# Odd rows of keys and queries copied inside SBUF, the first batch's value rows sent in two chunks, the first tokens by batch, a scaling moved to ScalarE, and a new order

## The chip, the cores and the metric

One core of a Trainium2 chip runs the kernel. The metric is the device time of one execution in microseconds (us); the time before is the median of three runs. The profile shows one further execution. Engines are named as the profile names them: PE (TensorE matmul), PEld (its weight load), DVE (VectorE), ACT (ScalarE), POOL (GpSimd) and SP (SyncE, which here issues every DMA).

## The reference

A gated linear recurrence with a complex decay, for 4 batches, 8 heads, 768 tokens and a head width of 48, followed by a two-layer network over the 3072 tokens:

```python
mag = np.sqrt(a_re * a_re + a_im * a_im)
scale = np.minimum(mag, 0.999) / (mag + 1e-06)
a_re_n, a_im_n = (a_re * scale, a_im * scale)
for t in range(S):
    ar, ai = (a_re_n[:, :, t, :, None], a_im_n[:, :, t, :, None])
    new_re = ar * S_re - ai * S_im
    new_im = ar * S_im + ai * S_re
    kv = np.einsum('bhd,bhe->bhde', k[:, :, t], v[:, :, t])
    S_re, S_im = (new_re + kv, new_im)
    y[:, :, t] = np.einsum('bhd,bhde->bhe', q[:, :, t], S_re)
# x = y as (4 * 768, 8 * 48)
h = x @ w_in                                     # 384 -> 2048
g = np.maximum(h, 0.0) + alpha * np.minimum(h, 0.0)
out = g @ w_out                                  # 2048 -> 384
```

## The kernel before

The recurrence is cut into 24 units of 128 tokens (4 batches of 6 chunks). The work is written as 15 + 24 generator tasks, each of which issues one instruction, or a small group, per step; a string of letters, `ORDER`, says which task takes the next step. So the order of every engine's queue, SP's included, is written out by hand in that string, and each engine runs its queue strictly in that order.

- A to I, `gates(g, b, c0, c1)`: from a_re and a_im the magnitude and phase of the decay for 128 tokens (g = 0), 256 tokens (g = 1) or 384 tokens (g = 2 to 8, 1152 elements in each of 128 partitions). It begins with L280, a scaling on DVE, and L282 to L286 on ACT; it goes on with products on DVE (L288 to L294), running sums (L307), more on both engines, and sends the phases to DRAM (L333, tensor phs) and, after L357 and the products of L367, the decays (L370, tensor decs).
- J, `loads`: for each unit the tile KQ. Its 96 partitions hold each of the 48 dimensions twice, in an even and in an odd row, so q and k are loaded twice from DRAM, with a step of two partitions: L508 (q) and L510 (k), 192 KB each, four loads a unit. Then PP from phs (L516) and T from decs, one load for the even rows and one for the odd (L523). KQ has three buffers, T two, PP one.
- K, `half_rows`: DRAM to DRAM copies of v with the rows apart that three of the levels need (tensor vsc, L489), six of 288 KB for each batch, each for all six chunks. L, `loads_v`: the tiles V (L532 to L537) and VL (L556 from v, L560 from vsc).
- M, `pieces`: the first token's keys of all batches (`start`, L405, single elements), alpha (L408), which DVE turns into al_1 at L410, and the weights as they come, in 16 pieces. N and O, `weights`: the pieces are 64-bit numbers that ACT (L444 to L448) and DVE (L452, L454) make into 32-bit ones.
- P to m, `unit(u)`: on DVE the rotation by the phases (L588, L590), then per level the decays (L646; the first of the six reads T and the rotated tile WQ, the others read T), on ACT copies of operands (L669, L685), on PE the small products (L605), masked on DVE (L629) or ACT (L619); then the state (L717 to L740; the first state of a batch at L654 reads `start`), and y on PE (L755, L769), which ACT copies out at L777. Units 0 and 1 go straight on to the network's tile xT (L786, L791); the others go through DRAM (L800, tensor ysc, and L817).
- n, `loads_x`; o, `all_mlp`: the network, 12 blocks of 256 tokens. Blocks 0 and 1 run plainly (L837 into L844 on ACT, L846 on DVE, L887); block 0 starts on unit 0's tokens alone. From block 2 on: L859 into L868 and L872 on ACT and L874 on DVE, then the seven products of a Strassen-like scheme (L977), whose weight combinations DVE makes at L943 and L952.

Of the kernel before, what the change touches and what calls it, by code (L numbers as in the profile page):

```python
# [27 lines left out]


ORDER = (  # L30
    "AAAAAMBMJMMBABABAAAAAAAAAAAAAJMBAAABBBMJJBAABAAKAAMAAAAAAAAAAAAABBBBNBBOBBBBBOBBONOJLOPBPPJLPJLLBBBL"
    "BNBPBBBBNBBBOBBBBPOPPPPJOPOPPPPBNNJLLJCCJJMBMKCPPNPCOCPQCKCNPJNNNPNPCQJLCPNPPPPPPPPPPPCQCCCCCNCPCQKL"
    "LKKMQQQPQLLLLOLJJJJJMCCNCCOOQQOCNNNQPPPPPPPPPQQQPCQCCLMQOQRPLLLLJoQooJMCLLLLCLCCCNRCoQooQoNRCCCCQoOQ"
    "QQQQooCooCQooNoDQRROoRCORRQQOQQDLLLRRLNLQDMJoCJOJQCCNRDNJQRRQQQOROOoQQQNOLLLOJLRRRDDDLoLooooooooQRRD"
    "QQooRRRRRRDNQooooRooRLJoLJooLRRDoNooooLoLRDRMRSRooDDSoooooooooooDoSDooooRLLRoLDSDRROSSSOoooooooLoOOS"
    "RRJSSOJJMRNoooooNooRJMSJLSSDoSNoooRooooSSSooooRooooOSDLLLLLMRSLRSSoDooooSSSSOSSoSoooOTOoooSSDOTooooo"
    "oooSSNSSDLNNNNNNNLooNNooSSMOLLLLLLJJOJJSoSSSJJoooSSSSSTLLJLnoooooooDLLTDJDOKTToTOooooooTTTLLODoooooT"
    "ooLDTTToLToDoDDDooooooooJJJJJooToTTTooDoUTTDUoLooTLoDLDDooUETTTLLLTToTooooJoTToTDTDDDTUEUUUUUUDDETTT"
    "ToooooUooEooTTTTTTETTUUooooULUVUUoLoooooooooUUoooUVUEUVLJJUJEVoJLooooooooUVUJUVUEooooLLLJLKJLKLVVVoV"
    "oUooVEooooooVooUooEUUUVVELUKLLVEVEoULUooooUUooEKKKKKUUWooVVVULUUULLoLLoooLVoVVEVJEoooJoLEVVVVoVVLLVE"  # L40
    "LooonLLLLoooEoVoLoVVWVEooJooooEJJJJVWKVEVVVWWWWEoWEWWWoVooVoVVVVVVoWLLWWWWELoWooooooooJooooooooLJLLL"
    "WWWWoEWLELJLoEooEWLLLWWooWWWoLLoooEXJEXXWoWoooWooXWWJXWWEWWXooooooooooooXXEXJJooXooWooWFFEEEEEEEEXoo"
    "ooooWooooooWWooWWXWXXXoooooooXLLooooooooLooooXJFoJXXLXXXXXXooYYYooooooXXXLooooooXoXooXYoYYYoonYKLLLL"
    "LLLLLLoYJYXXJXXoooooooYooooooooooooooooYFJYXXYoooXFJJKFFoooXooKXooXLLoYYYLoFXXXLXLLooooooFoFLFLoKYYY"
    "YYYYYLLLLLLJZoooooZooooooooJooYoYYFoLooYoooFYoYYoFFYFFFFFFFZYooooooooooYJoooYYoFYoFFYZFoJJJooJYooFYY"
    "YYYoZZZLLoooLooZJoooZZFJaZooooooooooLLZZZaFFFFooonoZZaZFFFaGooLLooooooooooooooooooooooooZZaZZZZZaFaZ"
    "ZaoooLooGJLLLLLoooooLLZZoJoooooZaZoooZJoZFGZaZooaoGJFGGFFFJFooooooooooooooZoZGZGoZoooZGGooooKooZooZZ"
    "ZLZZoooooooooooabaaGLLbaobLoGoooaLoooooaLLLLooooooLoooGaGaaoaaaaaGoooooooooooaaKoJJJobbooJLLaaLaoooo"
    "obGabbaaaaooLoobGbJbGGJbaoooJoaoaoobaaaaacoobbbbbooGbooooLcoooooooooobbbbbbbGooobJJbooLLLLLooncLLLLb"
    "boLooooooboooooobbGLLbbLGcooooGoooKocLJcJJJJGGGGGccbGbcbbcooooooooooGooooooooooooocGobooooboooobcccb"  # L50
    "bcdbbboooooooooooooooooocLLoooooccccooooooJLGooococccoJJLLLLHLLcccJcLLLLLLoooocooccddGdGdcHdcccccHGG"
    "GGodHoodoooooooooGGJoooHddoodoooooooooooocococoJcccccLdoJLJJJJJodddddooHHHoooooooooooooooodddddddddo"
    "ooeooeHoooeodHodooooooooLooooooodooooLJddddddeeedeendooLLoHHHLLLLLLLLHHHHLeeoooooooooooooooooooooood"
    "ooooedHededeedddJLLLdooooooooooooooooooooLeeeeHeooeooeeLLeHLLooooooooofeeeeoooeooLHJeeofeeHeooLLLLLe"
    "HoJHHLoooooJJJJJooHoHHeeHHoooeoffooooefeffHeeeeefffooofoooooooooJooLooooHffLooffffooooJoooooooooogoH"
    "oofffooffnHJooJHgHgfffLfooooooffIHJooooooLLLLLooooooooooHofgfoooooLLLLHLLHLHHfffgJgffffgggoooooooooo"
    "ooooJfooooooooofoooIgogfooooooIofgfgfffgooooooohgIggoooooooooIoooogIgoooogggIgIggJgooghgJooooLoooohh"
    "ooooohoooooggLLLLLLLLooggghhhhhooLJooIohooohLLLJLhggIooogoIgooJJJghhggggghonihIIooJJoooIooooooooohho"
    "ooooIoLLKLLooooooooooihhhJoJhhhhhIoIooIooIooohIohooooooooooLooooohhJiLhoooooooooLooooooooooooooiLLLL"
    "LLLLooohhihiIiiioJJhiiohhhohohooohiihLLLLLLihhiiiooooLooooooiiihihiiLLLLiiioooooooooooooiijooooiioIo"  # L60
    "ooooioooJoLLLLJooiiiiiIIiooooJjiIIIJJIIIIIooooooojoojoooooooJooooioooooJoiooojojjjIiiIIIoijiioooInjo"
    "ooooIoooooooooLjIIIkooooooooooLLLLLJLLLLojjjjjoooooJooooojoooooooLjjjoooooooooooooJoojjjjjjjkooooojo"
    "jjoooooooooJLoooookooojjjkkkjkjkLLjkjkLooooojoooJkjojJkkjjjLLjjJLLLLJkJLLkkoooooooooookkkkkkoookkooo"
    "okkoooookLLLLLLkooooookkoLookoolkkklollooooJokooJoooooookkJJJllkolllllookoooooooooooooookllkokkkklll"
    "LlooooooooooollllllLlloooooooolommonlJJlmoooooooooLLLLLooooooooooooooooooLLLLLLLloooooollllLlmoloooo"
    "oooooooooollmommlooolmmooolmmmmmlloommmoooooooooooooLLLLoooolmmmmoooloLLLLLLoommmmlooomomLLmoooooLLo"
    "ooooooooooooommooomommooooommoooooomomoomommmmmnoooooooooooooooooooooooooooooooooooooooooooooooooooo"
    "oooooooooooooooooooooooooooooooooooooooooooooooooooooooooooooooooooooooooooooooooooooooooooooooooooo"
    "oooooooooooooooooooooooooooooooooooooooooooooooooooooooooooooooooooooooooooooooooooooooooooooo")
# [28 lines left out]
def kernel(  # L98
# [145 lines left out]
    def gates(g, b, c0, c1):  # L244
# [35 lines left out]
        nc.vector.tensor_scalar(out=d, in0=x, scalar1=1.5, scalar2=TINY, op0=ALU.mult, op1=ALU.add)  # L280
# [119 lines left out]

    def pieces():

        t = yield DMA(8)
        with nc.allow_non_contiguous_dma(reason="one token"):
            nc.sync.dma_start(start[0:D2:2], kv_in[:, :, :, 0].rearrange("b d h -> d b h"))  # L405
        done["start", 0] = t
        t = yield DMA(8)
        nc.sync.dma_start(al_1, alpha)  # L408
# [68 lines left out]
    def half_rows():  # L477

        one = NCH * D2
        for b in range(B):  # L480
# [12 lines left out]
    loaded = {}

    def loads():
        for u in range(NU):
# [4 lines left out]
            n = min(P, S - 1 - c * P)
            if n < P:
                nc.gpsimd.memset(KQ[:, 1, :, n:P], 0.0)
            for i in range(2):
# [5 lines left out]
                nc.sync.dma_start(KQ[rows, 1, :, 0:n], kv_in[b, :, :, c * P + 1:c * P + 1 + n])  # L510
# [650 lines left out]
```

## Time and profile before

| what | value |
|---|---|
| time before, median of 3 runs | 763.77 us (761.33 to 764.42) |
| time of the profiled execution | 760.66 us |
| its span, first to last instruction | 758.6 us |
| PE busy | 682.7 us (90% of the span) |
| DVE busy | 605.5 us (80%) |
| ACT busy | 491.5 us (65%) |
| DMA packets | 175548, 129.82 MB, mean 171 GB/s |

The span is what the profile shows; 2.1 us of the profiled execution's time lie around it. A busy PE is not a PE at its peak: its matmuls are pipelined. The views used are the page, the table of busy times by stretch of the span, the waits (who waited for whom), the groups of instructions by line and shape, and the timeline of one engine.

### The profile page before, as it was taken

The page shows a single profiled execution, that of the slowest core. Times are in us where ns is not written, and L with a number is a line of the kernel's source. Part 1 is how long each engine was busy: PE and PEld are TensorE (multiplying, and loading weights), DVE is VectorE, ACT ScalarE, POOL GpSimd, SP SyncE. Part 2 cuts the span into 40 slices and gives each one's busy share as a digit, 9 for nine tenths or more (in the row PEclk, how much of TensorE's full clock was granted, in tenths as well). Part 3 has the DMA queues.
Part 4 walks back from the last instruction along what each step waited for, and adds up shares of the span by engine and source line. Part 5 has one row for each costly group of instructions (what it writes and reads, how often), then busy time and mean ns, then how long its engine had stood idle before and what let it go on. Part 6 is the DMA issues. An engine that isn't in the chain of part 4 may idle for free.

```text
span 758.6 us, 26858 instructions
## 1 busy us (share of the span) xinstructions
PE 682.7 (90%) x11752; PEld 581.3 (77%) x11752; DVE 605.5 (80%) x798; ACT 491.5 (65%) x887; POOL 13.0 (2%) x51
## 2 busy tenths in 40 slices
PE   0026789999999999999999999999999999999998
PEld 0015577776767888888888888988888988888987
DVE  6899999998999799998887997888876866742323
ACT  7979988965767678766856668565766455353330
POOL 5000000000000000000000000000000000000000
PEclk9998699999999999999999999999999999999999
DMA  9898999898678768667586648754744645211000
GB/s 243 252 318 242 283 242 224 217 267 232 189 187 232 219 158 179 206 187 160 140 207 203 172 91 217 218 127 118 191 122 141 190 113 143 74 45 52 1 22 21
DMA packets 175548, 129.82 MB, mean 171 GB/s; under 512 B 66184, under 2 KB 166792, under 8 KB 174984
## 3 DMA queue, kind: packets, MB, share of 16 engines
q1 hardware_dynamic: 175432, 128.12, 63.3%
q8 instruction: 92, 1.51, 0.8%
q14 instruction: 24, 0.20, 0.1%
HBM read 100.13 MB, written 35.02 MB: 178 GB/s over the span
## 4 chain that ended last, share of the span: by engine, by line
PE 70%; DVE 12%; DMA 7%; ACT 4%; SPq 4%; issue 3%; POOL 0%; DVEq 0%; ACTq 0%; POOLq 0%
PE ps_h L859 27%; PE ps_o L977 24%; PE ps_y L769 5%; PE ps_lv L605 5%; DVE KQ L646 3%; PE ps_y L755 2%; PE ps_kv L729 2%; DMA V<-in_v_dram 2%; SPq L556 2%; PE ps_kt L717 1%; DMA T<-decs 1%; DMA decs<-room 1%; PE ps_h L837 1%; PE ps_h L977 1%; DMA shared<-in_w_out_dram 1%
## 5 line engine op out<-in xcount | busy, mean ns | idle before, releaser
L859 PE MATMUL ps_h<-xT,w_in_sb 128*128 128x256 f32 x960 | 232.3, 385 | 0.0
L859 PEld LDWEIGHTS ps_h<-xT,w_in_sb 128*128 128x128 f32 x960 | 175.1, 190 | 21.9
L646 DVE TENSOR_TENSOR KQ<-KQ,T 96x1024 f32<-96x1024 f32 x120 | 145.9, 1216 | 31.9 <-PE ps_lv L605 25.4
L977 PE MATMUL ps_o<-w_out_sb,shared 128*128 128x192 f32 x624 | 113.1, 331 | 0.4 <-ACT top L993 0.4
L868 ACT ACTIVATE shared<-ps_h 128x512 f32<-128x512 f32 x80 | 47.8, 598 | 98.5 <-PE ps_h L859 98.2
L874 DVE TENSOR_TENSOR shared<-shared,ps_h 128x512 f32<-128x512 f32 x80 | 54.5, 682 | 68.6 <-ACT shared L872 68.6
L977 PEld LDWEIGHTS ps_o<-w_out_sb,shared 128*128 128x128 f32 x624 | 101.8, 190 | 3.4 <-ACT top L993 0.7
L977 PE MATMUL ps_o<-shared 128*128 128x192 f32 x448 | 84.0, 333 | 0.0
L872 ACT ACTIVATE shared<-shared,al 128x256 f32<-128x256 f32 x160 | 73.7, 502 | 2.4
L977 PEld LDWEIGHTS ps_o<-shared 128*128 128x128 f32 x448 | 72.8, 190 | 3.1 <-DVE top L1004 0.2
L605 PE MATMUL ps_lv<-WQ 96*32 96x32 f32 x2304 | 34.7, 202 | 38.6 <-DVE WQ L588 29.9
L605 PEld LDWEIGHTS ps_lv<-WQ 96*32 96x32 f32 x2304 | 26.3, 115 | 52.9 <-DVE WQ L588 29.9
L669 ACT COPY WQ<-KQ 96x1024 f32<-96x1024 f32 x48 | 49.8, 1039 | 26.2 <-DVE KQ L646 25.9
L769 PEld LDWEIGHTS ps_y<-A,VL 64*48 64x48 f32 x2304 | 39.9, 122 | 21.1 <-issue 17.6
L887 PE MATMUL ps_o<-w_out_sb,shared 128*128 128x384 f32 x128 | 52.5, 513 | 1.4 <-DVE shared L846 1.4
L769 PE MATMUL ps_y<-A,VL 64*48 64x64 f32 x2304 | 52.1, 225 | 1.7 <-DMA VL<-vsc 1.7
L837 PE MATMUL ps_h<-xT,w_in_sb 128*128 128x256 f32 (+1 forms) x240 | 52.3, 350 | 0.8 <-ACT xT L791 0.8
L837 PEld LDWEIGHTS ps_h<-xT,w_in_sb 128*128 128x128 f32 x240 | 41.1, 197 | 13.0 <-ACT xT L791 1.1
L685 ACT COPY W<-KQ 96x512 f32<-96x512 f32 x48 | 30.7, 640 | 26.4 <-DVE KQ L646 24.9
L619 ACT ACTIVATE A<-ps_lv,columns 128x64 f32<-128x64 f32 x144 | 36.8, 335 | 14.9 <-PE ps_lv L605 14.8
L777 ACT COPY T<-ps_y 48x512 f32<-48x512 f32 x48 | 27.8, 579 | 22.4 <-PE ps_y L769 21.7
L605 PE MATMUL ps_lv<-KQ,W 96*32 96x32 f32 x1536 | 24.3, 204 | 17.5 <-ACT W L685 17.5
(111 smaller groups left out, 962.7 us busy)
## 6 DMA issues: line engine op xcount, KB each, us to landing
T<-decs SPq DMA_DIRECT2D x48, 384.0 KB, 4.7
PP<-phs SPq DMA_DIRECT2D x24, 387.0 KB, 5.4
KQ<-in_q_dram SPq DMA_DIRECT2D x48, 192.0 KB, 5.6
phs<-room SPq DMA_DIRECT2D x14, 577.5 KB, 4.6
decs<-room SPq DMA_DIRECT2D x7, 1152.0 KB, 6.0
KQ<-in_k_dram SPq DMA_DIRECT2D x40, 192.0 KB, 4.8
vsc<-in_v_dram SPq DMA_DIRECT2D x24, 288.0 KB, 7.1
VL<-vsc SPq DMA_DIRECT2D x48, 144.0 KB, 3.9
```

The lines of the kernel that those rows point to most:

```text
L605: nc.tensor.matmul(t[64 * i + j:64 * i + j + HC // 2, p], lhsT=keys(n, g), rhs=queries(n, g), start=True, stop=True)
L619: nc.scalar.activation(a[:, :, cols], t[:, :, at:at + name], AF.Copy, scale=s)
L646: nc.vector.tensor_tensor(out=x, in0=x if x0 is None else x0, in1=m, op=ALU.mult)
L669: nc.scalar.copy(z.rearrange("p i n t -> p i (n t)").rearrange("p i (m h) -> p m i h", h=h), bass.AP(tensor=KQ.tensor, offset=KQ.offset + ...
L769: nc.tensor.matmul(o, lhsT=Vp[h][64 * i:64 * i + 64, s, e_ * D:(e_ + 1) * D], rhs=a, start=False, stop=(s == 1 and h == LEVELS[-1]))
L837: nc.tensor.matmul(p, lhsT=w_in_sb[:, f // 2, kk, f % 2 * P:(f % 2 + 1) * P], rhs=x_of[m][:, kk, c * P:(c + n) * P], start=(kk == 0), stop ...
L859: nc.tensor.matmul(p[:, i], lhsT=w_in_sb[:, f // 2, kk, i * P:(i + 1) * P], rhs=x_of[m][:, kk], start=(kk == 0), stop=(kk == NK - 1))
L868: nc.scalar.activation(gt, p, AF.Relu, scale=-1.0)
L872: nc.scalar.activation(some_, some_, AF.Copy, scale=al_1[:, f + i:f + i + 1])
L874: nc.vector.tensor_tensor(out=gt, in0=gt, in1=p, op=ALU.add)
L887: nc.tensor.matmul(sums[0], lhsT=gt, rhs=w_out_sb[:, f], start=(f == start), stop=(f == stop))
L977: nc.tensor.matmul(z, lhsT=a[:, i], rhs=w[:, i], start=i == 0, stop=i == F2 - 1)
```

## The change

Five edits:

- `loads`: for every unit but the first, only the even rows of KQ are loaded from DRAM (q and k, 192 KB each); when both have landed, one DMA of 384 KB copies the even rows to the odd rows inside SBUF.
- `half_rows`: for the first batch the copies are made for chunks 0 and 1 first and for chunks 2 to 5 later, twelve DMAs in place of six; units 0 and 1 then wait for the first six alone.
- `pieces`: the first token's keys are loaded for batch 0 alone at the start and for batches 1 to 3 after the second pair of weight pieces.
- `gates`: the scaling that opens a gate group is made on ACT, with the same result, for the seven groups g = 2 to 8.
- `ORDER` is another string, with 3878 letters in place of 3894.

```diff
-        t = yield DVE(N // 2, tx)
-        nc.vector.tensor_scalar(out=d, in0=x, scalar1=1.5, scalar2=TINY, op0=ALU.mult, op1=ALU.add)
+        if g < 2:
+            t = yield DVE(N // 2, tx)
+            nc.vector.tensor_scalar(out=d, in0=x, scalar1=1.5, scalar2=TINY, op0=ALU.mult, op1=ALU.add)
+        else:
+            t = yield ACT(N, tx)
+            nc.scalar.activation(d, x, AF.Identity, scale=1.5, bias=bias_tiny)
...
-        t = yield DMA(8)
-        with nc.allow_non_contiguous_dma(reason="one token"):
-            nc.sync.dma_start(start[0:D2:2], kv_in[:, :, :, 0].rearrange("b d h -> d b h"))
-        done["start", 0] = t
+        def first_tokens(b0, b1):
+            t = yield DMA(8)
+            with nc.allow_non_contiguous_dma(reason="one token"):
+                nc.sync.dma_start(start[0:D2:2, b0:b1], kv_in[b0:b1, :, :, 0].rearrange("b d h -> d b h"))
+            return t
+
+        done["start", 0] = yield from first_tokens(0, 1)
...
+            if f == 1:
+                t = yield from first_tokens(1, B)
+                for b in range(1, B):
+                    done["start", b] = t
...
-            for i, h in enumerate(SPREAD):
-                for s in range(HP // 2):
-                    rows = v[b, 2 * s]
-                    src = bass.AP(tensor=rows.tensor, offset=rows.offset + one, ap=[[2 * h * one, P // h], [1, h * one]])
-                    end = yield DMA(150)
-                    nc.sync.dma_start(vsc[s, i].rearrange("n (m h) c e -> (n m) (h c e)", h=h), src)
-            for c in range(NCH):
-                done["halves", b * NCH + c] = end
+            for c0, c1 in ((0, MC), (MC, NCH)) if b == 0 else ((0, NCH),):
+                for i, h in enumerate(SPREAD):
+                    for s in range(HP // 2):
+                        rows = v[b, 2 * s]
+                        src = bass.AP(tensor=rows.tensor, offset=rows.offset + one + c0 * D2,
+                                      ap=[[2 * h * one, P // h], [one, h], [1, (c1 - c0) * D2]])
+                        end = yield DMA(150)
+                        nc.sync.dma_start(vsc[s, i].rearrange("n (m h) c e -> (n m) h c e", h=h)[:, :, c0:c1].rearrange(
+                            "m h c e -> m h (c e)"), src)
+                for c in range(c0, c1):
+                    done["halves", b * NCH + c] = end
...
-            yield DMA(196, takes=(R["KQ"],))
+            tq = yield DMA(196, takes=(R["KQ"],))
...
-            for i in range(2):
+            for i in range(2 if u == 0 else 1):
...
                 nc.sync.dma_start(KQ[rows, 1, :, 0:n], kv_in[b, :, :, c * P + 1:c * P + 1 + n])
+            if u > 0:
+                t = yield DMA(393, tq, t)
+                nc.sync.dma_start(KQ[1:D2:2], KQ[0:D2:2])
...
-            k_ = yield DVE(H * D, k_, ("start", 0))
+            k_ = yield DVE(H * D, k_, ("start", b))
```

Counted in the two programs, SP issues 678 DMAs in place of 694 (KQ: 50 loads and 23 copies in place of 96 loads; vsc 30 in place of 24; `start` 2 in place of 1), DVE 791 instructions in place of 798 and ACT 894 in place of 887. PE issues the same matmuls in another order, which changes from one kind of matmul (a unit's small products, transposes, states, y, and the network's) to another 414 times in place of 425. Relative to the other queues' order, the first copy of y (L777) has on ACT one each of L444, L446, L448 and L685 less ahead of it, and one scaling more. On DVE, the first L874 has the same instructions ahead of it as before, less three L280.

More of the change, by code (lines that the diff above doesn't have):

```diff
@@ L36 @@
[L36 to L45, printed above, removed]
@@ L66 @@
[L66 to L67 removed]
+    "AAAAABMMAMBKMMBBAAAAAAAAABNMJJKAAAAAAAAJKJBBBAAAAAAAABMBAAAAALLAAAAAAJBBBBBBOBBBBBOBONOOBBPPKPPJJMBB"
+    "BBLLLLBBCNNNBPMBLBBBBPPPPPJLJNNBNPOOBNPNBCBBBPCJOPPPPPLOPOCCCNKPPPPPPPPPPPCCCLPPPPCJCCMNCJJKQPQCPQCC"
+    "COQCQQQJMLCPQCLLLLJNQCOOMKQKCCNNOPPPPPPJPPPJLQQCCPQQQKMLLLJJLCCCLCCONQQRRooooCooQQQNCooQoCooooNNRNLC"
@@ new lines @@
+    "CCLoQQQQQQQOORooooQooQoRRRMOJLRoQRQOLJDLLRLLLOQMNNNoooooooooRKoDDDoCCCJJQNNCRoQDDQQQQRQQRQRRDoRLoooD"
+    "QoooOoOOQoOOoQoRRooooLCRRRRLLLLLooRRooooLMoJoRRRSSooooRRooRRDNooJoRDDooooooooNNRSNNoDooRLoKLKLMLSORR"
+    "SooSOoSoooDLLLJJSSSMDooooooooNSRoooRSSNNNMRRoRJJRoRRooLLLLLDSSSoOLONSoOOooooooJSSJSoooooTSSLLSSSOLLL"
+    "LSSSSSoOLLLODToJoJSoDNNSOooTSTDNNDDSooooooooSDTTTTMSSSSSSSSSNSoLooTTOoooOooLDnOOOTooooooooooTTTLJDJT"
+    "JDDDLLLLLLTDJooooooooTDUDDLDLJJLLoooUooDoooTTTToTDooDDoooooooTTToTToDUDooTToToTTTTUUUUTTTDLLoooooUTo"
@@ new lines @@
+    "UUDDEJJooUToooTUDUTTTUooooUUUKDVLLLTTVEEELoooooooooEEoLUUUUUUUUooooLLLVoUUEEEooUoJVoooUUooooUoJUUEEo"
+    "ooooooooVEEEEEVEULLLLLLUVoVVoUUKKoKEJJVKKKUoJVVEoUUULooooooUUVVVVoooooVVVooLJLLooooooooVJJLLLLLLLVLL"
+    "LLVnooVVVVVVVVVooooJJoEWWoVVWEJVVVWWWWWWVVVooJoVVoVWEWWWVVVVVLLLoWoWEEWJJJJWoLLLLooooooooooooooooooo"
+    "oEWWWXXXELEEEEoWWLJLooooWWWWEoWWoooooooooooWooLooWLLLWWXoLXooXooooWWWEEEEEEoooEooooooXoXKJEFWWoooEoo"
+    "oooWoWoXooXXoWoWEWWWWXXXXYXoXooooooooooooooooooXLnJJXLLXXXooooLLXoooooYYoXXXXXoooooooKXoLLLLLFLLLXLL"
@@ new lines @@
+    "YooFoXXXXXJYYXXJKooYYFoYFoYoooooooooooooooFKFFXoJXoXXooJooXXFYLFXXooooooLooooYYJJYZYFYYooooooooooooo"
+    "FooooooooYJYYYFYYYYooYoZYFYoZooooooYooooooLLLKYLYYZoYYZLLLLLFFLLZFFZJZZFYFFFYFZYLLJJooooooooooooYoYo"
+    "YYYYYYFLLLLJLJooooooooFLLLnLFZFLooooooFFFZZZZaZZoooooooooooooooooaFLLoFZZZoooLooooooFFooZooooooZZZZZ"
+    "ZZoFoaFFooooooooGLLoZGJooJKZZZFZZFFoaaaaaZoZZKKooFooooooGoGGGaooZooooooaZoooooooooKaGoooooooJoZJaaFZ"
+    "ZKGaZZaaaobooooooooooooooooaaaoaaoGoGoZLGoLLLLaaaaobbooooooaooJJoooooooooaGLLabbooaLLLLLLbababaaaoob"
@@ new lines @@
+    "bbbGGobGoGooLooaoGooaoabbaGaaJJJJaaJooLbboGoooobnLbLLLooooooooooooobbbooobbGLJooobbbbbbocoGocbbLLLLL"
+    "LLLLGooooooooooGoooooobbbcbGJJGGGGbcoooooooooooJJGGooooooobGbcccoccGobcocooooooooooooGobcbcbbboLcccb"
+    "bcodHoooooooooooooooooocccdoccccooocoGGcoooHooooHJJGcoooGLLcooocHocooGdcccddLKdddcoHccJcddooHoooLoJo"
+    "LLLLLLJGoooooLLLLooGGooHHHHoooooooooooodcooHcoocdddcHHHdcccddcJoHooooooJLoLJoooooooooddLLodHHddddooo"
+    "JooHHeHHooLednLLLLedddoooLLLLoooooooooooooodooodLoLoodddeddHeeddeooHHHooooeHHoeeHooooooooooooooooooo"
@@ new lines @@
+    "odHJJooododHeeedeLeoooooooddddoooLJooooooLoooeeeeJJeeeoooHoooLLoHoooooofffoeeeoeeooeoeeLLLLLLLLLLooo"
+    "ofoooooooefJeeeJJeHHeeooooooooooooooooIefffeoofooooooooooooeffffIJfHHHeeeeeJfffoooooJooHnooooooooooo"
+    "oofffgofgIfoooofHffooofffoooLLgoHooooHoooJfoofLoLLLLIgIoooooooooLLLLoLLLLfffffggggffIooooJHooooooooo"
+    "JJoooooIgggfIoooooooooooooooooofgfgfffghhgoghgoooooooooffooooLLLooooLoggghIIggoJooooooooooooooooLLgJ"
+    "ggggJoooLLLgogIgooLLgghhhhLLLJgggJhJhhhIIIooooooooooooIoohgooIIghghgIhhIoggggoJJoJoooohooooonoIiiJLh"
@@ new lines @@
+    "LLooooooooooooooooooooIoooIiLLLLLLLLLLoooooiLooooooooohhhhhhhhiiiihooooooooooooooJhoooooohhioooooohh"
+    "LhhIihIIIIooohoooooIihhooooohIIiIhihohiiiihhohhLLoLoooooLiLiiiioooLoooooLooiiJJLoIooIIIIoiiioLLJJJoL"
+    "LLLoooooIIoooooooooooLIIoooooJjjoooooooooooooJooooiioojojiiiiojjiijiioooooIjoiooijoojoijjjjiiiiijjjn"
+    "LkoooooooooooooooLoLLLojjojjjjjjJLjLLLLLoLLLoooooojJjoJJooooooooooooooojjooooooooooooooooooooookokko"
+    "oooooooooojjjkkLjkjjjkkooJoooookkojojoojkkkJjjjjjkkkoooooooooolkkkkkkooookkoooLooLLoLLLLLLkkkooooooo"
```

31 lines of the change are left out of this document (5 added, 26 removed).

## The prediction

> **What bounds the kernel now.** I read the profile's page first, for the shape of the run, and then cut the span into the stretches that the page's digits suggest.
>
> ```profile
> span 758.6 us, 26858 instructions
> ...
> PE   0026789999999999999999999999999999999998
> ...
> DVE  6899999998999799998887997888876866742323
> ```
>
> Each digit is the busy share of 19 us. PE has next to nothing to do in the first 38 us and is full from about the seventh slice; DVE is full from the second slice to about the twelfth. The busy times by stretch (columns: length, then busy us and instructions of PE, its loads, DVE, ACT, POOL, then granted clock, DMA share, GB/s) put numbers on it:
>
> ```profile
> 0.00:76.00 76.00, 17.85 (x532) 15.19 (x532) 64.91 (x101) 65.56 (x91) 11.15 (x35) 0.96 0.91 263
> 76.00:100.00 24.00, 18.42 (x449) 14.59 (x449) 23.79 (x36) 23.67 (x37) 0.00 (x0) 0.76 0.97 291
> 100.00:260.00 160.00, 151.88 (x2822) 115.80 (x2823) 147.34 (x193) 115.42 (x220) 0.79 (x5) 1.00 0.86 225
> 260.00:700.00 440.00, 439.80 (x7649) 384.49 (x7648) 350.60 (x441) 274.48 (x518) 1.09 (x11) 1.00 0.58 150
> 700.00:759.00 59.00, 54.74 (x303) 51.25 (x301) 18.84 (x30) 12.38 (x25) 0.00 (x0) 1.00 0.04 14
> ```
>
> From 260 us on PE is busy 494.5 of 499 us, and the change takes no matmul away. So nothing that happens there to DVE, ACT or the DMAs can pay, except by harm; the end moves by as much as PE's full stretch moves to the left. PE stands idle 58.2 us before 76 us, 5.6 us from there to 100 us and 8.1 us from there to 260 us. In the same stretches DVE is busy 64.9 of 76, 23.8 of 24 and 147.3 of 160 us: the head is DVE's, with ACT as full beside it from 76 to 100 us. The hand-over lies where the network's later blocks begin, at the first L874 on DVE:
>
> ```profile
> 227.29 0.67 DVE L874 TENSOR_TENSOR shared<-shared,ps_h 128x512 f32<-128x512 f32 x1
> ```
>
> I therefore ask of each edit how much earlier it lets DVE reach this instruction, and whether it makes DVE wait on the way.
>
> **The scaling on ACT.** Its rows, with those of the ACT work that I need next (columns: count, busy us, mean ns, idle before):
>
> ```profile
> L280 DVE TENSOR_SCALAR room<-room 128x1152 f32<-128x1152 f32 x4 | 3.0, 748 | 0.0
> L319 ACT ACTIVATE room<-room,columns 128x1152 f32<-128x1152 f32 x3 | 3.8, 1256 | 0.0
> L444 ACT ACTIVATE top<-shared 128x768 f32<-128x768 f32 x16 | 14.4, 906 | 0.6 <-DVE w_in_sb L454 0.6
> L446 ACT ACTIVATE w_in_sb<-shared,columns 128x768 f32<-128x768 uint32 x8 | 7.9, 992 | 0.0
> L448 ACT ACTIVATE w_in_sb<-shared 128x768 f16<-128x768 f32 x8 | 8.5, 1068 | 0.1
> L685 ACT COPY W<-KQ 96x512 f32<-96x512 f32 x18 | 11.5, 641 | 12.2 <-DVE KQ L646 10.8 <-DVE room L367 1.3
> ```
>
> The instructions that stand on DVE ahead of the first L874 are the same in both orders but for three L280: 3 × 0.748 = 2.2 us off the engine that sets the head. ACT takes them as L319's kind, Identity with a bias: 3 × 1.256 = 3.8 us more. From 100 to 260 us ACT has 44.6 us free, so two of the three are covered; the one that falls in the full stretch up to 100 us costs between 0 and 1.3 us, and I take 0, since the order also takes ACT work out of that place. Without that cover the 2.2 us would shrink to about 0.9.
>
> **The order.** The first copy of y on ACT opens the network's work:
>
> ```profile
> 71.20 1.17 ACT L777 COPY T<-ps_y 48x512 f32<-48x512 f32 x2
> 76.25 0.79 PE L837 MATMUL ps_h<-xT,w_in_sb 128*128 128x128 f32 x2 [0.84 <-ACT xT L791]
> ```
>
> ACT's queue ahead of it loses one each of L444, L446, L448 and L685 and gains a scaling: 0.906 + 0.992 + 1.068 + 0.641 − 1.256 = 2.4 us. On DVE, the eighth L846 has one each of L292, L294, L588, L646, L737 and L740 less ahead of it, besides two scalings, so PE gets more of block 0's features before 100 us. But those six are only put behind, and the first L874 has them ahead of it again. What the order can win there is DVE's waiting, not its work. Between 0 and 2.4 us; I take 1.0 us, nearer the low end, since DVE has only 0.2 us of idle from 76 to 100 us.
>
> **The first tokens.** The start of SP's queue, and what waits for it:
>
> ```profile
> 1.83 0.73 SPq L405 DMA_DIRECT2D start<-in_k_dram  x1
> 2.60 1.16 SPq L272 DMA_DIRECT2D room<-in_a_re_dram  x1
> 3.81 0.48 SPq L408 DMA_DIRECT2D al<-in_alpha_dram  x1
> ```
>
> ```profile
> 4.99 0.52 ACT L286 ACTIVATE room<-room 128x384 f32<-128x384 f32 x1
> 7.10 0.17 DVE L410 TENSOR_SCALAR al<-al 128x16 f32<-128x16 f32 x1 [2.63 <-DMA al<-in_alpha_dram]
> ```
>
> L288, the first gate group's next step, was ready at 4.99 + 0.52 = 5.5 us but stands on DVE behind L410, which waits for alpha. With `start` for one batch issued behind a_re, alpha's turn on SP comes at about 1.83 + 0.48 + 0.73 = 3.0 us in place of 3.81: 0.8 us, and everything in the head follows from this group. The bounds are 0 (the second a_re then ends the wait) and 7.1 − 5.5 = 1.6 us; I take 0.8. The other batches' keys, and v in chunks, are wanted later or no sooner than before: the last of the six vsc DMAs that units 0 and 1 need stands at the same place of SP's queue as all six did, before unit 0's VL. I cost them at nothing; the cover is that place, and if it were gone PE's y would wait for one more DMA to land, up to the 7.4 us of the longest such landing quoted below.
>
> **The copy inside SBUF.** No such DMA is in this trace. T's load from the profile's page (issues, KB each, median us from issue to landing), and the landing times of all of KQ's loads:
>
> ```profile
> T<-decs SPq DMA_DIRECT2D x48, 384.0 KB, 4.7
> ```
>
> ```profile
> DMA to landing us min/median/max: 3.4/5.2/7.4
> ```
>
> ```profile
> 64.34 0.62 SPq L510 DMA_DIRECT2D KQ<-in_k_dram  x1
> 77.45 1.21 DVE L588 TENSOR_TENSOR WQ<-KQ,PP 96x1024 f32<-96x1024 f32 x1
> ```
>
> By its size the copy is nearest to T's load, 4.7 us; the bounds are KQ's own shortest and longest, 3.4 and 7.4 us. Unit 2 shows the cover: k issued at 64.34, landed 5.2 us later, copy issued in 0.62 us and landed 4.7 us after that is 74.9 us, 2.6 us ahead of L588; with 7.4 us it is 77.6 us, just late. So nothing is lost on DVE while k stands where it stood, and I take 0. If the cover is gone, L588 waits, and all of DVE's queue with it. SP issues two loads less and one copy more a unit, 0.62 us each; a gain from that is excluded in the full stretch by PE's 439.8 of 440 us. The Trainium skill's page "DMA: Bandwidth & Descriptors" (Anatomy of one DMA) fits 2.0 us plus bytes over 436 GB/s; for 384 KB that would be an estimate of 2.9 us, and the copy would land at 73.1 us, which leaves the sum as it is. No run shown here has this copy.
>
> **The sum.** 2.2 + 0.8 + 1.0 = 4.0 us earlier, from 760.66 us of the profiled execution (span 758.6) to 756.7. The median of the runs is 763.77, 3.1 us above that execution, and my forecast stands on the median: 759.8 us. With all terms at their ends it is from 757.6 (2.2 + 1.6 + 2.4) to 762.9 (0.9 alone). About 0.5%, 3.8 us, is what a measurement of this kernel can tell from no change, so the forecast itself lies at that edge.
>
> **Rivals.** First, slower: SP stops at each copy until q and k have landed, and what stands behind comes late.
>
> ```profile
> SPq L800 <- ACT T L777: 91.7, 33, 9.2
> ...
> SPq L523 <- DMA decs<-room: 8.7, 3, 6.6
> SPq L523 <- DMA ysc<-T: 8.0, 8, 2.9
> ...
> DVE KQ L646 <- DMA T<-decs: 6.0, 6, 2.2
> ```
>
> In 15 of the 23 units at most three issues stand between the load of k and the copy, so SP stops there for about 5.2 − 2 × 0.62 = 4.0 us. In 12 units the first load of T stands at most eight issues behind the copy. T comes just in time already: SP holds it for its buffer, and DVE has waited for it six times. If each of these 12 units lost 1 us of PE, the time would be 759.8 + 12 = 772 us. It decides where SP's stop runs past the moment at which T's buffer comes free. Against it: SP stands 91.7 us at L800 anyway, so the queue as a whole is not short of time. The Trainium skill's page "DMA: Bandwidth & Descriptors" (Rules for kernel authors) demands exactly this wait: a DMA that reads what another wrote must wait for the first one's completion. The trace agrees on its price for another pair, 6.6 us at L523 behind decs.
>
> Second, a larger gain: PE's clock.
>
> ```profile
> 40.00:50.00 10.00, 2.63 (x128) 2.09 (x128) 8.85 (x11) 7.94 (x10) 0.00 (x0) 1.00 1.10 315
> 70.00:80.00 10.00, 7.30 (x117) 6.33 (x118) 10.00 (x13) 9.86 (x13) 0.11 (x1) 0.53 0.83 244
> ```
>
> ```profile
> 79.31 1.62 PE L837 MATMUL ps_h<-xT,w_in_sb 128*128 128x128 f32 x6
> ...
> 98.36 0.83 PE L837 MATMUL ps_h<-xT,w_in_sb 128*128 128x128 f32 x6
> ```
>
> Six equal matmuls take 1.62 us at the low clock and 0.83 us later. From 76 to 100 us the clock is 0.76 of full with PE busy 18.42 us: 4.4 us lost. If the earlier and denser network work kept the clock up, the time would be 759.8 − 4.4 = 755.4 us. The Trainium skill's page "TensorE: Matmul & The Clock Gate" (Part 1: The HAM clock gate) says that the throttled clock is the default and activity releases it. By that rule this happens; the trace agrees only in part, with 1.00 beside 2.63 us of work in 10 and 0.53 beside 7.30.
>
> Third, nothing: DVE is full behind the earlier network work too, PE gets its work sooner and waits for units later, and ACT's extra 1.3 us lies in the way: 763.8 to 766, say 764.5 us.
>
> **How the numbers follow.** Forecast 0.42, of which two thirds are beyond the edge; larger gain 0.16; nothing 0.18; slower 0.24. Faster by over 0.5%: 0.28 + 0.16 = 0.44. Within: 0.14 + 0.18 = 0.32. Slower: 0.24. The range from 753 (the second rival with both ends of my terms, 757.6 − 4.4) to 773 us (the first) leaves out units that lose more, about a sixth.
>
> **What would show it.** In the changed kernel's profile: L410 waits about 0.8 us less; the first L874 at about 223 us; the first L837 near 74 us; PE idle before 260 us down from 71.9 to about 68 us, and PE as full as now from there on. I am wrong if SP's waits for KQ's loads at the copy come back as waits of DVE at L588 or L646, or of PE at L605, or if PE shows idle time after 260 us.

## The result, and the profile after

The changed kernel takes 757.0 us (median of 6 runs, 754.79 to 758.97) beside 763.8 us for the kernel before on the same chip (6 runs, 761.33 to 766.89): a ratio of 0.9915, 95% interval 0.9889 to 0.9942, that is 4.4 to 8.5 us less. The forecast was 4.0 us less. The profiled execution took 758.25 us, at the slow end of its six, and the one of before, 760.66 us, was faster than all six of its runs beside it; so the two traces differ by 2.4 us where the medians differ by 6.8, and sizes below rest on ratios, the traces only on where.

From the page of the changed kernel: span, and the tenths of PE and DVE in 40 slices of 19 us.

```profile
span 755.8 us, 26824 instructions
...
PE   0035889899999999999999999999999999999998
...
DVE  5999999998999799988999986898976756832323
```

PE's digits are higher in the third and the fifth slice and lower in the fourth and the eighth. The busy times by stretch (columns as in the prediction) say what it comes to:

```profile
0.00:76.00 76.00, 19.60 (x540) 16.65 (x540) 65.36 (x102) 66.94 (x93) 11.43 (x35) 1.00 0.97 262
76.00:100.00 24.00, 18.39 (x439) 14.87 (x440) 23.40 (x36) 23.48 (x39) 0.00 (x0) 0.86 1.03 282
100.00:260.00 160.00, 154.54 (x2841) 118.00 (x2840) 147.74 (x192) 120.35 (x224) 0.54 (x5) 0.99 0.81 222
260.00:700.00 440.00, 437.43 (x7647) 385.50 (x7646) 347.13 (x436) 276.38 (x517) 1.18 (x11) 1.00 0.57 152
700.00:757.00 57.00, 51.98 (x289) 48.75 (x287) 18.40 (x29) 11.83 (x25) 0.00 (x0) 0.99 0.04 14
```

PE stands idle 260 − 19.60 − 18.39 − 154.54 = 67.5 us before 260 us, where it was 71.9. From 260 to 700 us it stands 2.6 us, where it was 0.2: over half of these 4.4 us is given back. DVE is no emptier before 260 us (236.5 us busy, 236.0 before).

The timeline at the places that the prediction named:

```profile
6.45 0.17 DVE L417 TENSOR_SCALAR al<-al 128x16 f32<-128x16 f32 x1 [1.95 <-DMA al<-in_alpha_dram]
7.01 0.79 DVE L292 TENSOR_TENSOR room<-room 128x384 f32<-128x384 f32 x1
72.45 1.36 PE L854 MATMUL ps_h<-xT,w_in_sb 128*128 128x128 f32 x8
227.18 0.68 DVE L891 TENSOR_TENSOR shared<-shared,ps_h 128x512 f32<-128x512 f32 x1
```

L417 was L410: its wait fell from 2.63 to 1.95 us. The network's first matmul (L854, was L837) starts at 72.45 instead of 76.25. L292, the first gate group's next step (was L288), starts 0.64 us earlier, at 7.01 instead of 7.65. But the hand-over on DVE (L891, was L874) is at 227.18 instead of 227.29: not the 4 us earlier that I had forecast.

The copy inside SBUF, from the page's DMA issues, the landing times of the copy's line, and the waits (us in total, times, longest):

```profile
T<-decs SPq DMA_DIRECT2D x48, 384.0 KB, 4.3
KQ<-KQ SPq DMA_DIRECT2D x23, 384.0 KB, 4.5
```

```profile
DMA to landing us min/median/max: 3.8/4.5/5.1
```

```profile
SPq L817 <- ACT T L794: 101.5, 39, 11.2
...
SPq L527 <- DMA KQ<-in_k_dram: 40.1, 17, 4.5
...
DVE KQ L663 <- DMA T<-decs: 6.0, 4, 3.2
```

It lands in 4.5 us (I took 4.7), and SP stops for it 17 times, 40.1 us in all. DVE waits for T no longer than before, 6.0 us in all: in this order the stops don't come back as waits of DVE.

### The profile page after: what moved, and what is told of

It reads as the page before. It is cut to its first block, busy times and chain, and to the rows that moved or that the text cites. A ratio compares the mean times of both kernels' runs of the same rounds, so it can differ in the third digit from the quotient of the medians.

```text
span 755.8 us, 26824 instructions
## 1 busy us (share of the span) xinstructions
PE 681.9 (90%) x11752; PEld 583.8 (77%) x11752; DVE 602.0 (80%) x791; ACT 499.0 (66%) x894; POOL 13.1 (2%) x51
## 4 chain that ended last, share of the span: by engine, by line
PE 81%; DMA 7%; ACT 5%; DVE 4%; issue 2%; SPq 1%; POOL 0%; ACTq 0%; DVEq 0%; POOLq 0%
PE ps_h L876 28%; PE ps_o L994 23%; PE ps_y L786 6%; PE ps_lv L622 6%; PE ps_o L904 5%; PE ps_h L854 4%; PE ps_kv L746 3%; DMA T<-decs 3%; PE ps_y L772 3%; PE ps_kt L734 2%; PE ps_h L994 1%; DMA KQ<-in_k_dram 1%; DVE KQ L663 1%; DMA shared<-in_w_in_dram 1%; DMA VL<-vsc 1%
## 5 line engine op out<-in xcount | busy, mean ns | idle before, releaser
L663 DVE TENSOR_TENSOR KQ<-KQ,T 96x1024 f32<-96x1024 f32 x120 | 146.0, 1217 | 34.7 <-PE ps_lv L622 26.0
L994 PE MATMUL ps_o<-w_out_sb,shared 128*128 128x192 f32 x624 | 115.1, 331 | 0.9 <-issue 0.5
L891 DVE TENSOR_TENSOR shared<-shared,ps_h 128x512 f32<-128x512 f32 x80 | 54.4, 682 | 63.1 <-ACT shared L889 62.8
L994 PE MATMUL ps_o<-shared 128*128 128x192 f32 x448 | 81.9, 331 | 0.0
L854 PE MATMUL ps_h<-xT,w_in_sb 128*128 128x256 f32 (+1 forms) x240 | 53.6, 352 | 4.0 <-issue 3.3
L786 PE MATMUL ps_y<-A,VL 64*48 64x64 f32 x2304 | 53.8, 226 | 1.5 <-issue 0.8
L854 PEld LDWEIGHTS ps_h<-xT,w_in_sb 128*128 128x128 f32 x240 | 41.3, 199 | 12.8 <-ACT WQ L686 1.3
```

The source lines that it names most:

```text
L663: nc.vector.tensor_tensor(out=x, in0=x if x0 is None else x0, in1=m, op=ALU.mult)
L786: nc.tensor.matmul(o, lhsT=Vp[h][64 * i:64 * i + 64, s, e_ * D:(e_ + 1) * D], rhs=a, start=False, stop=(s == 1 and h == LEVELS[-1]))
L854: nc.tensor.matmul(p, lhsT=w_in_sb[:, f // 2, kk, f % 2 * P:(f % 2 + 1) * P], rhs=x_of[m][:, kk, c * P:(c + n) * P], start=(kk == 0), stop ...
L891: nc.vector.tensor_tensor(out=gt, in0=gt, in1=p, op=ALU.add)
L994: nc.tensor.matmul(z, lhsT=a[:, i], rhs=w[:, i], start=i == 0, stop=i == F2 - 1)
```

## Experiments

All ratios are to the kernel before, run beside them on the same chip; a kernel's own time moves from chip to chip with that of before (763.3 to 765.7 us). The ± of a difference of two ratios is the root of the sum of the squares of the two half-widths. Two questions were open: which edit carries the gain, and by what.

**One part undone or done alone.** First the scaling back on DVE, in the new order:

```diff
-        if g < 2:
+        if True:
             t = yield DVE(N // 2, tx)
```

> The changed kernel with the scaling of all gate groups on DVE again; order and DMAs as changed. The prediction's account (three scalings of 0.748 us off the engine that sets the head): the changed kernel's 757.0 becomes 759.2 us, and PE's busy time before 260 us falls by about 2 us. Rival, PE's clock and PE's own queue set the head: within 1 us of 757.0.

Measured: 763.85 us, ratio 0.9985 (0.9962 to 1.0008). Most of the gain is gone, 0.0070 ± 0.0035 or 5.3 ± 2.7 us, where my account had 2.2. The trace shows one place where it goes. ACT's timeline of this kernel, then that of the changed kernel at the same place of the program (fourth gate group after g = 0):

```profile
179.73 1.05 ACT L686 COPY WQ<-KQ 96x1024 f32<-96x1024 f32 x1
185.12 1.16 ACT L286 ACTIVATE room<-room 128x1152 f32<-128x1152 f32 x1 [4.35 <-DVE room L281]
186.31 0.38 ACT L861 ACTIVATE shared<-ps_h 128x256 f32<-128x256 f32 x1
```

```profile
175.15 1.05 ACT L686 COPY WQ<-KQ 96x1024 f32<-96x1024 f32 x1
176.11 1.25 ACT L284 ACTIVATE room<-room,columns 128x1152 f32<-128x1152 f32 x1
177.39 1.16 ACT L286 ACTIVATE room<-room 128x1152 f32<-128x1152 f32 x1
178.58 0.38 ACT L861 ACTIVATE shared<-ps_h 128x256 f32<-128x256 f32 x1
```

In the changed kernel ACT does the scaling in 1.25 us and goes on, past L286, to L861, the network's step behind PE's matmuls. With the scaling on DVE, ACT stands 4.35 us at L286, because DVE has other work ahead of it, and L861 stands behind. DVE then waits for L861, and PE for DVE:

```profile
186.73 0.48 DVE L863 SCALAR_TENSOR_TENSOR shared<-shared,al,ps_h 128x256 f32<-128x256 f32 x1 [1.64 <-ACT shared L861]
187.26 1.13 PE L854 MATMUL ps_h<-xT,w_in_sb 128*128 128x256 f32 x4 [1.26 <-DVE shared L863]
```

The waits of the whole run:

```profile
ACT room L286 <- DVE room L281: 15.4, 6, 6.6
```

Without the first two groups, which scale on DVE in both kernels, that is 12.2 us in four places. The hand-over comes at 234.34 us, 7.2 later than in the changed kernel, and the span is 7.2 us longer (763.0; this execution, 765.91 us, was the slowest of its twelve). These 7.2 us don't all come from that wait. Beside the changed kernel, the first of a unit's decays (L663) starts 0.4 us later in unit 2, 2.9 in unit 3, 5.1 in unit 5 and 7.7 in unit 6. The last step, 2.6 us, stands at the 4.35 us wait. The step at unit 3 comes where ACT had waited only 0.66 us, and where the granted clock from 104 to 108 us was 0.51 beside 1.00 in the changed kernel; what made it, and the step at unit 5, is not shown.

Next, the odd rows from DRAM again, at the copy's step:

```diff
-                nc.sync.dma_start(KQ[1:D2:2], KQ[0:D2:2])
+                odd = slice(1, D2, 2)
+                nc.sync.dma_start(KQ[odd, 0], qv[b, :, :, cols])
+                nc.sync.dma_start(KQ[odd, 1, :, 0:n], kv_in[b, :, :, c * P + 1:c * P + 1 + n])
```

> The changed kernel with the odd rows of q and k loaded from DRAM, two loads at the step where the copy stood, not waiting for the even rows; order, scaling, v and first tokens as changed. The prediction's account (copy costed at nothing): 757.0 us within 1 us. Rival, relief of the DMA engines (92 in place of 100 MB read from HBM, shorter landings) carries the gain: 759 us or more, with the landing of T, V and VL as long as before (4.7, 6.2, 3.3 us). Rival, SP's stops at the copy cost something: 756 us or less.

Measured: 759.05 us, ratio 0.9928 (0.9898 to 0.9958), 0.0013 ± 0.0040 above the changed kernel and so not to be told from it, nor from the rival's 759 us; this trace gives no landing times of T, V and VL to compare. HBM reads are back at 100.13 MB; 9 MB less to read is worth 1 ± 3 us, nothing that shows. In this run's profile PE's clock stays at full speed:

```profile
76.00:100.00 24.00, 19.38 (x439) 15.36 (x439) 23.18 (x36) 23.39 (x39) 0.00 (x0) 1.00 1.09 268
```

The new order with no other edit has the two diffs above and the two of the small edits below, together. The old order with all edits keeps the string of before, and its steps are matched so, beside the changed kernel:

```diff
-            t = yield DMA(8)
+            t = (yield DMA(8)) if b0 == 0 else None
...
-                        end = yield DMA(150)
+                        end = (yield DMA(150)) if b or s % 2 == 0 else None
...
             if u > 0:
+                yield DMA(1)
                 t = yield DMA(393, tq, t)
```

> The new order with none of the four other edits: scaling on DVE, first tokens whole at the start, odd rows from DRAM at the copy's step, the first batch's v whole on the first six of its twelve steps. The prediction's account (order 1.0 of 4.0 us): 762.8 us. Rival, the order carries the gain (PE busy earlier, at a higher clock): 758 to 759 us with a granted clock of about 0.86 from 76 to 100 us.

> The order from before with all four edits: scaling on ACT, first tokens by batch, odd rows copied inside SBUF at the step of the fourth load, the first batch's v in two chunks, two DMAs a step. The prediction's account (scaling 2.2, alpha 0.8): 760.8 us. Rival, the order carries the gain: 763 to 764 us, with the granted clock from 76 to 100 us near 0.76. Rival, SP's stop at the copy hurts where the order was not made for it: over 764.5 us, with waits at T's loads.

Measured: the order alone 763.5 us, ratio 0.998 (0.9958 to 1.0002); the edits alone 775.54 us, ratio 1.0141 (1.0103 to 1.018). Neither part shows a gain by itself. In the order alone ACT waits for DVE's scaling as above (16.3 us, 6 times), and the same 4.35 us wait goes with 2.8 us more lateness at unit 6.

**Why the old order loses.** The kernel before with one edit each: the copy, with the odd rows' two loads left out and the copy at the second one's step,

```diff
-            for i in range(2):
+            for i in range(2 if u == 0 else 1):
...
+            if u > 0:
+                yield DMA(1)
+                t = yield DMA(393)
+                nc.sync.dma_start(KQ[1:D2:2], KQ[0:D2:2])
```

and the scaling, with the diff of the change:

> The kernel before, its order kept, with one edit: the odd rows of q and k are copied inside SBUF at the step of the fourth load (the third step issues nothing). All four edits in that order gave 1.0141 of the time before. Theory, SP's stop at the copy delays T where the order was not made for it (the prediction's slower rival): 770 us or more, with DVE waiting over 4 us for T's loads before 260 us. Rival, another of the edits did the harm: 764 us within 2.

> The kernel before, its order kept, with one edit: the scaling of gate groups 2 to 8 on ACT. The prediction's account (DVE's work ahead of the hand-over): 2.2 us less, 761.6. The account by waits (in the trace of before ACT waits 6.8 us in three places for DVE's scaling, which goes where both steps stand on ACT): 757 to 760 us. Rival, the order must fit: 763 us or more.

Measured for the copy: 774.02 us, ratio 1.0134 (1.0106 to 1.0162). This is the slower rival of the prediction, which had 772 us for it. SP's and DVE's waits in this run:

```profile
SPq L804 <- ACT T L781: 71.0, 30, 8.7
...
SPq L514 <- DMA KQ<-in_k_dram: 58.5, 19, 4.8
```

```profile
DVE KQ L650 <- DMA T<-decs: 15.3, 12, 2.6
```

SP stops 58.5 us at the copies, and DVE waits 12 times for T, 15.3 us, where the trace of before has 6 times and 6.0 us: 9.3 us more, close to the 10.2 us that the copy costs. What I see different from the new order is how far T is ahead of its use. Unit 3's T and the first instruction that reads it, here and in the changed kernel:

```profile
110.91 0.60 SPq L527 DMA_DIRECT2D T<-decs  x1
```

```profile
116.34 1.22 DVE L650 TENSOR_TENSOR KQ<-WQ,T 96x1024 f32<-96x1024 f32 x1 [1.51 <-DMA T<-decs]
```

```profile
103.65 1.28 SPq L540 DMA_DIRECT2D T<-decs  x2
...
113.95 1.22 DVE L663 TENSOR_TENSOR KQ<-WQ,T 96x1024 f32<-96x1024 f32 x1
```

The last load goes out 5.4 us ahead of its use in the old order and 9.6 in the new (113.95 less about 104.3, where the second load starts). Unit 3 is among the clearest. Over the first ten units the median of this margin is 5.7 us in this run, 6.2 in the kernel before and 7.4 in the changed kernel; over all 24 it is 6.6, 6.8 and 7.1. No run moves T alone, so that the margin decides is argued, not shown. The counts of the prediction don't tell the orders apart: 15 of 23 copies stand close behind k in both, and T close behind the copy in 12 units in the new order and 10 in the old.

Measured for the scaling in the old order: 764.77 us, ratio 1.0007 (0.9985 to 1.0029). Nothing, and here my expectation misread a row. The trace of before does show ACT waiting 6.8 us for DVE's scaling in three places, but two of these are the first groups, which stay on DVE. The third, 2.74 us, is group 7 at 402 us, long after the hand-over. In groups 2 to 4 it doesn't wait:

```profile
7.77 0.85 ACT L282 ACTIVATE room<-room 128x768 f32<-128x768 f32 x1 [2.26 <-DVE room L280]
...
45.47 1.16 ACT L282 ACTIVATE room<-room 128x1152 f32<-128x1152 f32 x1
92.73 1.16 ACT L282 ACTIVATE room<-room 128x1152 f32<-128x1152 f32 x1
170.89 1.17 ACT L282 ACTIVATE room<-room 128x1152 f32<-128x1152 f32 x1
```

In that order DVE comes to these scalings in time, and the edit, 2.2 us off DVE's head and 3.8 us more on ACT, comes to 0.5 ± 1.7 us more. It doesn't tell the two sides apart.

**The small edits undone**, the first tokens whole at the start, and v whole on the first six steps:

```diff
-                nc.sync.dma_start(start[0:D2:2, b0:b1], kv_in[b0:b1, :, :, 0].rearrange("b d h -> d b h"))
+                if b0 == 0:
+                    nc.sync.dma_start(start[0:D2:2], kv_in[:, :, :, 0].rearrange("b d h -> d b h"))
```

```diff
+                w1 = NCH
...
-                                      ap=[[2 * h * one, P // h], [one, h], [1, (c1 - c0) * D2]])
+                                      ap=[[2 * h * one, P // h], [one, h], [1, (w1 - c0) * D2]])
                         end = yield DMA(150)
-                        nc.sync.dma_start(vsc[s, i].rearrange("n (m h) c e -> (n m) h c e", h=h)[:, :, c0:c1].rearrange(
+                        if c0:
+                            continue
+                        nc.sync.dma_start(vsc[s, i].rearrange("n (m h) c e -> (n m) h c e", h=h)[:, :, c0:w1].rearrange(
```

> The changed kernel with the first tokens of all batches loaded by the first DMA again, the later step issuing nothing. The prediction's account: alpha's wait grows by 0.65 to 0.8 us and everything with it, 757.7 us. Rival, the other work in the head swallows it: 757.0 within 0.4 us.

> The changed kernel with the first batch's v copied whole, six DMAs of 288 KB on the first six of its twelve steps, the other six steps issuing nothing. The prediction's account (chunks costed at nothing): 757.0 us within 1. Rival, unit 0 waits for the longer copies: PE's first y 1 to 3 us later and 758 to 760 us.

Measured: 758.7 us, ratio 0.9939 (0.9914 to 0.9963), and 758.93 us, ratio 0.9949 (0.9925 to 0.9974). Both lie above the changed kernel's 0.9915, and neither clearly. The traces show the mechanisms at their places, alpha's first:

```profile
7.20 0.17 DVE L418 TENSOR_SCALAR al<-al 128x16 f32<-128x16 f32 x1 [2.69 <-DMA al<-in_alpha_dram]
```

```profile
65.72 2.87 PE L789 MATMUL ps_y<-A,VL 64*48 64x64 f32 x80 [2.06 <-DMA VL<-vsc]
...
73.76 1.65 PE L857 MATMUL ps_h<-xT,w_in_sb 128*128 128x128 f32 x6
```

With `start` whole, alpha comes 0.75 us later (7.20 beside 6.45), though its turn on SP is the same. Its own issue takes longer behind the whole `start`, here first and then in the changed kernel:

```profile
3.12 1.19 SPq L416 DMA_DIRECT2D al<-in_alpha_dram  x1
```

```profile
3.13 0.60 SPq L415 DMA_DIRECT2D al<-in_alpha_dram  x1
```

With v whole, PE waits 2.06 us for VL where the changed kernel waits 0.66, and the network begins 1.3 us later.

**DVE's time, ACT's wait, and POOL.** Is DVE's busy time worth anything in the new order? First, work of its own added on DVE:

```diff
             nc.scalar.activation(d, x, AF.Identity, scale=1.5, bias=bias_tiny)
+            for _ in range(4):
+                nc.vector.tensor_scalar(out=idle, in0=idle, scalar1=1.5, scalar2=TINY, op0=ALU.mult, op1=ALU.add)
```

> The changed kernel with nothing moved, and four scalings of a small tile of their own (96 elements a row, nobody waits for them) added on DVE where each scaling of groups 2 to 8 stood, 0.6 to 0.8 us for each of the seven places: the busy time of the old scaling without any other engine waiting for it. Putting the scalings themselves back on DVE gave 763.85 us. The prediction's account (only DVE's busy time ahead of the hand-over counts, three places): 759.2 us, so that over half of the 5 us lies in ACT's waiting for DVE's turn. Rival, DVE's busy time is all of it: 762 us or more. Third, DVE's time costs nothing here: 757 us.

```profile
L288 DVE TENSOR_SCALAR idle<-idle 128x96 f32<-128x96 f32 x28 | 5.8, 208 | 0.7
```

Measured: 759.14 us where before took 765.71, ratio 0.9912 (0.9878 to 0.9945). Four times 0.208 us at each of seven places, more than the 0.748 us of a scaling, cost nothing that shows. The difference to the changed kernel is −0.2 ± 3.3 us, so the 2.5 us of the three places ahead of the hand-over aren't excluded.

Second, one product of each gate group on POOL, in all groups and in the first three:

```diff
-        TT(out=rows3(c), in0=y, in1=rows3(c), op=ALU.mult)
+        nc.gpsimd.tensor_tensor(out=rows3(c), in0=y, in1=rows3(c), op=ALU.mult)
...
+        (nc.gpsimd if g < 3 else nc.vector).tensor_tensor(out=rows3(c), in0=y, in1=rows3(c), op=ALU.mult)
```

> The changed kernel with one product of each gate group (a_im times the sine, 1.35 us on DVE for 1152 elements a row) on POOL, beside DVE's other product. If DVE's time in the head counts as the scaling's did, 2.2 us or more of it off DVE before the hand-over gives 752 to 755 us. Rival, POOL takes over twice as long or slows DVE while it works, and DVE waits for it: 758 us or more.

> As the run before, with the product on POOL only in the gate groups 0 to 2, which lie ahead of 100 us. If DVE's time in the head counts: 754 to 756 us. Rival, POOL's longer time delays the first groups' chain and everything after it: 758 to 762 us.

```profile
L319 POOL TENSOR_TENSOR room<-room 128x1152 f32<-128x1152 f32 x7 | 19.4, 2769 | 248.7 <-DVE room L311 62.4 <-ACT room L314 56.8 <-DMA PP<-phs 47.0
```

Measured: 765.93 us, ratio 0.9994 (0.9969 to 1.0018), and 760.02 us, ratio 0.9934 (0.9907 to 0.996). The first is slower although 10.9 us of products leave DVE. POOL's product takes 2.77 us against DVE's 1.35, and DVE is slower while POOL works:

```profile
197.75 3.15 POOL L319 TENSOR_TENSOR room<-room 128x1152 f32<-128x1152 f32 x1 [32.23 <-ACT room L314]
```

```profile
198.53 3.45 DVE L663 TENSOR_TENSOR KQ<-KQ,T 96x1024 f32<-96x1024 f32 x1
```

Such an L663 takes 1.22 us in the changed kernel. Beside each of the seven products of 1152 elements a row one DVE instruction took 2.65 to 3.53 us in place of 0.55 to 1.22, and DVE's busy time as a whole rose from 602.0 to 609.7 us. So the edit takes nothing off DVE; the rival that POOL slows DVE came true. How the loss divides between this and POOL's longer time was not taken apart.

Last, the scaling on DVE but early enough: issued by the loop over `ORDER`, 2 to 10 DVE instructions ahead of its own step.

```diff
+            if i in EARLIER:
+                self.early.pop(EARLIER[i])()
```

> The changed kernel with the scaling of gate groups 2 to 8 on DVE, each issued 2 to 10 DVE instructions ahead of its own step, so that DVE has done it about 3 us before ACT comes to the step behind it; the order and all else as changed. At its own step the same scaling on DVE gave 763.85 us, 0.9985 of the time before, with ACT 12.2 us in wait for it. Account by ACT's waits: 0.991 to 0.993 of the time before, as the changed kernel. The prediction's account (DVE's busy time, 2.2 us): 0.9944. Rival, the new order only fits ACT: 0.997 or more.

```profile
ACT room L296 <- DVE room L269: 4.0, 3, 1.8
```

Measured: 759.59 us, ratio 0.9944 (0.9922 to 0.9966). This is the figure that the prediction's account gave; the one by ACT's waits, 0.991 to 0.993, is missed, though the interval still holds its upper end. ACT's wait for the scaling is down from 15.4 to 4.0 us (3.4 in the changed kernel, all of it in the first two groups), and of the 0.0070 that the scaling cost at its own step 0.0041 ± 0.0032 is back, without a change of DVE's work. At unit 6, where the same scaling at its own step cost 2.6 us, this trace shows no new lateness (0.5 us less than at unit 5). The rest, 0.0029 ± 0.0034 or 2.2 ± 2.6 us, may be DVE's 2.2 us, as my account had it, or nothing, as the middle of the run with added work has it; these runs don't settle it.

No variant beats the changed kernel; the one with DVE work added and the one with the odd rows from DRAM equal it within their intervals.

## Why the prediction was right or wrong

**The direction and the sum.** Forecast 4.0 us less, measured 4.4 to 8.5: right in kind, short in size. The median of 757.0 us lies below 757.6, the sum with every term at its best end, and inside the range only by the room that the clock rival had opened. PE's idle time before 260 us fell to 67.5 us, as forecast (68). The end did not move by as much in these traces: 2.3 us of idle came back behind 260 us, and the span is 2.8 us shorter. The medians differ by 6.8 us; where the rest lies, two traces that differ by so much less can't show.

**The scaling** is the term that was mis-sized: 2.2 us forecast, 5.3 ± 2.7 measured in the new order, no gain (0.5 ± 1.7 us more) in the old one. The step that failed is "the instructions that stand on DVE ahead of the first L874": I priced an engine's busy time alone. The runs show that ACT's waiting for DVE's turn is a part of it that I left out: 0.0041 ± 0.0032 of the 0.0070, or 3.1 ± 2.4 us, comes back when DVE does the scaling earlier. The trace of before doesn't show this wait at the three steps ahead of the hand-over, since that order let DVE come in time. The other 2.2 ± 2.6 us stay open. As I read it, the edit buys freedom for the order: the scaling can stand late, right ahead of the step on ACT that needs it.

**The hand-over** at about 223 us was wrong: 227.18 us, and 227.18, 227.38 and 226.30 in the runs with the odd rows from DRAM, the first tokens whole and DVE's work added. DVE did not reach it 4 us earlier, so the gain did not come on the path that the sum priced, and that the sum came near is in part luck. Between orders the hand-over isn't the measure that I took it for. In the trace of before PE still lost time behind it,

```profile
242.07 0.32 PE L769 MATMUL ps_y<-A,VL 64*48 64x64 f32 x6 [1.68 <-DMA VL<-vsc]
```

and the changed kernel's PE is busy without a break from 227 to 260 us. Within the new order it goes the right way, but not by the same size: 7.2 us later in the run with the scaling on DVE, with 7.2 us more span, but 3.1 us later in the run with the scaling early on DVE, with 6.5 us more span.

**The order**, 1.0 us: alone it gave 1.5 ± 1.7 us, which fits 1.0 and nothing alike, but it was no term to be added. It is the condition of the others: without it the scaling gives no gain and the copy costs 10.2 us.

**First tokens**, 0.8 us: alpha came 0.65 us earlier, but not by its turn on SP alone. In the two traces of the new order with `start` whole its turn is the same and it came at 7.09 and 7.20 us; in the eight with one batch at 6.29 to 6.58. Nor does everything in the head follow from this group: its product L319 (was L315) starts later than before, since the new order puts two other steps ahead of L314 on ACT, of which L455 waits for the weights. Before, then after:

```profile
12.20 0.53 DVE L315 TENSOR_TENSOR room<-room 128x384 f32<-128x384 f32 x1
```

```profile
11.90 0.89 ACT L455 ACTIVATE top<-shared 128x768 f32<-128x768 f32 x1 [0.88 <-DMA shared<-in_w_in_dram]
```

```profile
13.24 0.56 DVE L319 TENSOR_TENSOR room<-room 128x384 f32<-128x384 f32 x1 [1.59 <-ACT room L314]
```

Undone, the time rose by 1.8 ± 2.8 us, too wide to size it.

**v in chunks**, nothing: wrong in its place. I took the position in SP's queue as the cover; PE waits 1.4 us less for VL with the chunks. On the time, 2.6 ± 2.8 us.

**The copy**, nothing: right in the new order, with the landing 4.5 us, inside 3.4 to 7.4. The Trainium skill's page "DMA: Bandwidth & Descriptors" (Anatomy of one DMA) has its fit for DMAs issued by GpSimd; taken over to these copies of SP it gives an estimate of 2.9 us. All 23 copies took longer, 3.8 us at least.

**Slower rival:** its mechanism came true, DVE waiting for T behind SP's stops, and its price is near (12 us forecast, 10.2 measured), but only in the order from before. That 772 and 774.02 lie closer still is chance, since they start from different times. My count of issues could not tell the orders apart; how far T is ahead of its use in time goes the right way.

**Larger gain, PE's clock:** the clock from 76 to 100 us did rise, 0.76 to 0.86, but it can't be most of the gain. The three executions in whose traces it was 1.00 all through that stretch (odd rows from DRAM, v whole, and DVE's work added) took 758.52, 758.94 and 756.26 us, where the medians of the same kernels are 759.05, 758.93 and 759.14. Over 91 runs of the kernel before, taken chip by chip, 0.01 less mean clock goes with 1.1 us more (standard error 0.4); its mean was 0.989, that of the changed kernel's six runs 0.991: about 0.3 us. Why a low clock costs so little, these runs don't show.

**PE idle after 260 us**, named as a sign of being wrong, did come: 2.6 us beside 0.2 from 260 to 700 us. It is small beside the 6.8 us between the medians, but in these two traces it takes back over half of what PE won before 260 us, and the prediction had nothing for it. The other sign, SP's stops coming back as waits of DVE for T, came only in the old order.

## What to carry to other kernels

Price a step that moves between engines by who waits for it and what stands behind the waiting instruction, not by its busy time alone: 0.75 us on DVE held ACT's queue for up to 6.6 us. Where queues are in order and written out by hand, an edit has no worth of its own: the same copy cost 10 us in one order and nothing that shows in another, so an edit is judged after the order has been made for it. For a DMA that makes its queue stop, read the margin between the issue and the use of what stands behind it. And before an engine is called relieved, read its busy time after the change: POOL's help left DVE busier.

## What the runs showed of the hardware

- A 384 KB copy inside SBUF, 48 rows of 8 KB to 48 others, landed in 3.8 to 5.1 us, about as long as a load of the same size from DRAM (T, 4.3 us in the median).
- The first tokens' DMA of single elements took 0.73 us of SP's queue for one batch's keys as for four. What differed was the next issue, alpha's: 0.60 us behind one batch, 0.90 and 1.19 behind four in the two traces of the new order with `start` whole.
- A product of two tiles of 1152 elements a row took 1.35 us on DVE and 2.77 us on POOL, and one DVE instruction beside each such product on POOL took 2.65 to 3.53 us in place of 0.55 to 1.22.
- The kernel before ran with a mean clock between 0.978 and 1.000 from run to run, and 0.01 less went with little over 1 us more.
